# Packed turns of q, two loads behind a broadcast, and two reordered exps in a fused attention and feed-forward kernel

## The chip, the cores and the metric

The kernel runs on one core of one Trainium2 chip. The metric is the device time of an execution in microseconds (us). Engines are named as in the profile: PE is TensorE, PEld its weight loads, DVE VectorE, ACT ScalarE, POOL GpSimd, and SP the queue that issues transfers. A profile of one execution gives the span, from the first to the last instruction, which is some 2 us shorter than that time, and a trace of every instruction and transfer.

## The reference

Linformer attention (8 batches, 8 heads, 1024 rows, head size 64) feeds a maxout feed-forward block:

```python
k_proj = einsum('ks,bhsd->bhkd', E, k)          # 64 projected rows
v_proj = einsum('ks,bhsd->bhkd', F, v)
scores = q @ k_proj.T / 8
attn   = exp(scores - max); attn /= attn.sum(-1)
x      = (attn @ v_proj) -> [8192, 512]
h      = maximum(maximum(x @ w1, x @ w2), x @ w3)   # 512 -> 768
out    = h @ w_out                                   # 768 -> 512
```

## The kernel before

Instructions are issued in a hand-made order: while TensorE does the feed-forward of batch b, the attention of batch b+1 is slipped in between steps. A step (0, 3) is the fourth of ten in the first half of a batch; steps 0 to 5 are column groups of w1, w2, w3, steps 6 to 9 are output projections. PSUM has eight banks; `bank()` and `two()` hand out the bank (or pair) that the model of time thinks free first.

The parts that matter (cuts marked):

```python
def load(b, which):                      # q, k, v of batch b: float32 in HBM -> bf16, on the GpSimd queue
    ...
        dma = nc.gpsimd.dma_start(out=tiles[i], in_=view((q, k, v)[i], b))
        if i == 0 and b - 1 in last_T:   # q waits for the q transposes of the batch before
            after(dma, last_T[b - 1])

def heads_q(b, g, sis, t):               # turns of q for batch 0: half-width transposes on TensorE
    for i, si in enumerate(sis):
        for hp in range(2):
            nc.tensor.transpose(out=t[hp*HALF:(hp+1)*HALF, i*P:(i+1)*P],
                                in_=qkv[b][0][:, 2*g + hp, si, :], identity=ident)

def zc(b, queue=nc.sync):                # 1 / row sums of a whole batch
    ...  # sums on TensorE; Ln and Exp on ScalarE -> zic
        nc.sync.dma_start(out=zd..., in_=zic...)           # 32 KB to DRAM
        for u in range(2):
            for hp in range(2):
                queue.dma_start(out=zi_all(b)[...], in_=zd[gs, hp].partition_broadcast(HALF))

def qd(b, parts=1):                      # q of the other batches: packed on VectorE, turned by DMA
    ...
        last_T[b] = nc.sync.dma_start_transpose(out=qTs[b][...], in_=q_p[...])

def sc(b, g, lo=0, nsi=SI, now=False):   # scores; the exp follows now, or after the next h1 copy
    ...
def up(b, ch, jt, mid=None):             # one column group of w1, w2, w3
    ...
    nc.scalar.copy(out=h1s, in_=h[0][0])
    run_later()                          # postponed exps
    nc.vector.tensor_tensor(out=m12, in0=h[1][0], in1=h1s, op=ALU.max)
    most(hTs[b, ch][:, jt, :], *h[2], m12)
```

`vx(b, g)` multiplies the values by `zi_all` into `xT`, the input of the feed-forward; `za` does sums, inverse and values of one head pair.

The softmax here doesn't subtract the row's maximum and nothing guards it: scores larger than these inputs give would overflow.

Of the kernel before, what the change touches and what calls it, by code (L numbers as in the profile page):

```python
# [15 lines left out]
def kernel(  # L16
# [231 lines left out]
    def zc(b, queue=nc.sync):  # L248



        def f():
            t, ns = bank()
            for hp in range(2):
                for g in range(NPAIR):
                    nc.tensor.matmul(  # L256
                        out=t[32 * g:32 * (g + 1), :], lhsT=pick[:, hp, :],
                        rhs=pTs[b, g, 0][:, hp, :], start=(hp == 0), stop=(hp == 1),
                    )
            ready = pe(2 * MM + 0.1)  # L260
            zlc = att.tile([P, CHUNK], FP32, name="zlc", bufs=1)
            nc.scalar.activation(out=zlc, in_=t, func=AF.Ln)
            runs("s", ready, 0.6, ns)
            zic = att.tile([P, CHUNK], FP32, name="zic", bufs=1)
            nc.scalar.activation(out=zic, in_=zlc, func=AF.Exp, scale=-1.0)
            when = runs("s", ready, 0.63) + 9.0
            zd = scratch.tile([NPAIR, 2, 2, CHUNK], FP32, name="zd")
            nc.sync.dma_start(
                out=zd.rearrange("g h c f -> (g h c) f"),
                in_=zic.rearrange("(a r) f -> a r f", r=8)[:, 0, :],  # L270
            )
            for u in range(2):
                gs = slice(2 * u, 2 * u + 2)
                for hp in range(2):
                    queue.dma_start(
                        out=zi_all(b)[hp * HALF:(hp + 1) * HALF, gs],
                        in_=zd[gs, hp].partition_broadcast(HALF),
                    )
            for g in range(NPAIR):
                zis[b, g, 0] = zi_all(b)[:, g], when  # L280
        return f
# [39 lines left out]
    def sc(b, g, lo=0, nsi=SI, now=False):  # L321
        def f():
            t = scores(b, g, lo, nsi)
            if now:
                exps(b, g, lo, nsi, t)
            else:
                later.append(lambda: exps(b, g, lo, nsi, t))
        return f

    def za(b, g, lo=0, nsi=SI, then=False):  # L330
        def f():
            z = sums(b, g, lo, nsi)
            av = values(b, g, lo, nsi)
            invert(b, g, lo, nsi, z)
            if then:
                later.append(lambda: scale_x(b, g, lo, nsi, av))
            else:
                scale_x(b, g, lo, nsi, av)
        return f
# [13 lines left out]
    def heads_q(b, g, sis, t):  # L353
        for i, si in enumerate(sis):
            for hp in range(2):
                nc.tensor.transpose(
                    out=t[hp * HALF:(hp + 1) * HALF, i * P:(i + 1) * P],
                    in_=qkv[b][0][:, 2 * g + hp, si, :],
                    identity=ident,
                )  # L360
        pe(0.08 * len(sis))

    def qp(b, gs, lo=0, nsi=SI):
        def f():
            if b not in qTs:
                qTs[b] = att.tile([P, NPAIR * SI, P], BF16, name="qT")
            t, ns = two()
            t = t.bitcast(BF16)[:, 0]
            n = nsi * P
            for i, g in enumerate(gs):  # L370
                heads_q(b, g, range(lo, lo + nsi), t[:, i * n:(i + 1) * n])
            o = qTs[b].rearrange("a (g si) p -> a g si p", si=SI)
            copy(
                "v", o[:, gs[0]:gs[-1] + 1, lo:lo + nsi, :],
                t[:, 0:len(gs) * n].rearrange("a (g si p) -> a g si p", si=nsi, p=P),
                ns, 0.1 + len(gs) * nsi * 0.08,
            )
        return f
# [20 lines left out]
    def kproj(b):  # L399
        def f():  # L400
            t, ns = bank()
            proj(b, 1, t, (LO, HI), 4 * D)
            kps[b] = att.tile([P, 2, 2 * D], BF16, name="kp")
            copy("v", kps[b].rearrange("a g x -> a (g x)"), t[:, 0:4 * D], ns, 0.43)
        return f
# [18 lines left out]
    def vproj(b):  # L424
        def f():
            t, ns = bank()
            proj(b, 2, t, (LO, HI), 4 * D)

            vps[b] = att.tile([P, H, D], BF16, name="vp")
            for hh, hs in enumerate((LO, HI)):  # L430
                i = t[hh * HALF:(hh + 1) * HALF, 0:4 * D].rearrange("a (h d) -> a h d", d=D)
                for to in range(2):
                    copy("sv"[hh], vps[b][to * HALF:(to + 1) * HALF, hs, :], i, ns, 0.4)
        return f
# [247 lines left out]
    def ld(b, which=(0, 1, 2)):  # L682
        return lambda: load(b, which)

    def plan(b):
        n = b + 1
        if b == 0:
            c1 = (SPC, SPC)
            return {
                (0, 6): [za(0, 1, *c1), sc(0, 3, *c1)],  # L690
                (0, 7): [qd(1, 2), za(0, 2, *c1)],
                (0, 8): [za(0, 3, *c1)],
                (1, 0): [kproj(1)],
                (1, 1): [kt(1)],
                (1, 2): [vproj(1), ld(2)],
                (1, (3, "mid")): [sc(1, 0), sc(1, 1)],
                (1, 4): [za(1, 0), sc(1, 2)],
                (1, 5): [za(1, 1), sc(1, 3)],
                (1, 7): [za(1, 2)],
                (1, 8): [za(1, 3)],  # L700
            }
        if b == 1:
            return {
                (0, 0): [qd(2)],
                (0, 3): [kproj(2), vproj(2), ld(3, (0, 1))],
                (0, 4): [kt(2)],
                (0, 5): [sc(2, 0, now=True), sc(2, 1, now=True), sc(2, 2)],
                (0, 6): [sc(2, 3)],
                (0, 8): [zc(2, nc.gpsimd), ld(3, (2,))],
                (1, 1): [qd(3)],  # L710
                (1, 3): [vx(2, 0), vx(2, 1)],
                (1, 6): [vx(2, 2), vx(2, 3)],
            }
        if b == 2:
            return {
                (0, 1): [kproj(3), vproj(3), ld(4)],
                (0, 2): [kt(3)],
                (0, 3): [sc(3, 0, now=True), sc(3, 1)],
                (0, 5): [sc(3, 2, now=True), sc(3, 3)],
                (0, 7): [zc(3)],  # L720
                (0, 8): [qd(4)],
                (1, 3): [kproj(4), vproj(4), ld(5), vx(3, 0), vx(3, 1)],
                (1, 4): [kt(4)],
                (1, 6): [vx(3, 2), vx(3, 3), sc(4, 0)],
            }
        if n == B:
            return {}
        out = {
            (0, 1): [sc(n, 1, now=True), sc(n, 2, now=True), sc(n, 3)],
            (0, 3): [zc(n)],  # L730
            (1, 2): [vx(n, 0), vx(n, 1)],
            (1, 6): [vx(n, 2), vx(n, 3)],
        }
        if n + 1 < B:
            out[0, 4] = [qd(n + 1)]
            out[1, 2] = [kproj(n + 1), vproj(n + 1)] + out[1, 2]
            out[1, 3] = [kt(n + 1)]
            out[1, 6] += [sc(n + 1, 0)]
        if n + 2 < B:
            out[1, 3] += [ld(n + 2)]  # L740
        return out

    for b in range(B):
        p = plan(b)

        def behind(ch, step):
            for f in p.get((ch, step), []):
                f()

        for ch in range(NCHUNK):  # L750
            if (b, ch) == (0, 0):
                c1 = (SPC, SPC)
                up_first({
                    (0, 0, 5): [lambda: v_pair(2)],
                    (0, 1, 2): [lambda: x(2)],
                    (0, 1, 5): [lambda: v_pair(3), ld(1)],
                    (0, 2, 2): [lambda: x(3)],
                    (2, "a", 2): [qp(0, (0, 1), *c1)],
                    (2, "a", 4): [qp(0, (2, 3), *c1)],
                    (2, 0): [sc(0, 0, *c1)],  # L760
                    (2, 2): [sc(0, 1, *c1)],
                    (2, 4): [za(0, 0, *c1, then=True), sc(0, 2, *c1)],
                })
                run_later()
                behind(0, NJT - 1)
            else:
                for step in range(NJT):
                    up(b, ch, step, lambda: behind(ch, (step, "mid")))
                    behind(ch, step)
            for tt in range(SPC):  # L770
                down(b, ch, tt, "v" if b == 0 else "s")
                behind(ch, NJT + tt)
# [30 lines left out]
```

## Time and profile before

Three executions took 403.04, 403.15 and 403.41 us; the profiled one took 402.78 and spans 401.0 us. This is the head of its page (busy time, share of the span, count) and the chain of waits by engine:

```profile
span 401.0 us, 5737 instructions
PE 388.7 (97%) x2261; PEld 176.7 (44%) x2303; DVE 203.3 (51%) x319; ACT 149.0 (37%) x238; POOL 34.1 (9%) x48
...
PE 80%; DMA 11%; DVE 3%; issue 2%; ACT 2%; POOL 1%; DVEq 0%; ACTq 0%; POOLq 0%
```

TensorE is busy 97% of the time, at a granted clock of 1.00. Only its waits can be won. From 28 us on, the view of waits of TensorE shows these (total, times, longest). A wait "on issue" of 0.16 us stands where a matmul record is missing, and is none.

```profile
PE banks L664 <- issue: 0.8, 5, 0.2
PE banks L567 <- issue: 0.8, 5, 0.2
PE banks L664 <- DVE hT L577: 0.7, 1, 0.7
PE banks L231 <- DVE xT L308: 0.3, 1, 0.3
PE banks L345 <- DMA v_t<-in_v_dram: 0.3, 1, 0.3
PE banks L567 <- DVE xT L308: 0.2, 1, 0.2
```

The largest, 0.7 us, is the end of a story that the timeline tells (start, duration, engine, operation; in brackets the idle time before it and what ended it; SPq and POOL lines are issues of transfers):

```profile
88.50 0.89 POOL L200 DMA_DIRECT2D k_t<-in_k_dram  x1
...
99.76 0.53 SPq L268 DMA_DIRECT2D zd<-zic  x1
104.81 2.58 POOL L275 DMA_DIRECT2D zi_all<-zd  x4 [15.42 <-DMA zd<-zic]
107.39 0.91 POOL L200 DMA_DIRECT2D v_t<-in_v_dram  x1
112.63 2.35 DVE L308 TENSOR_TENSOR xT<-banks,zi_all 128x1024 bf16<-128x1024 f32 x2 [1.70 <-PE banks L567]
117.83 0.39 PE L664 MATMUL banks<-wout_sb,hT 128*128 128x512 bf16 x1 [0.70 <-DVE hT L577]
```

A load of k occupies the DMA engines (16.0 us to landing); the tiny zd write needs 4.5 us; the broadcast starts late, so VectorE idles 1.70 us, then is late with hT.

Two more places, the turns of q with the first output projection, and the projection of v of batch 1. The first line, of a projection of v of batch 0, serves below as a mark:

```profile
20.52 0.61 PE L496 MATMUL banks<-v_t,efT 128*128 128x128 bf16 x8
...
33.02 0.64 PE L356 MATMUL banks<-ident,q_t 128*64 128x128 bf16 x16
33.59 1.04 PE L567 MATMUL banks<-xT,w_sb 128*128 128x512 bf16 x4
...
34.56 0.64 PE L356 MATMUL banks<-ident,q_t 128*64 128x128 bf16 x16
...
39.60 1.46 PE L664 MATMUL banks<-wout_sb,hT 128*128 128x512 bf16 x6
...
55.95 1.06 PE L345 MATMUL banks<-v_t,efT 128*64 128x256 bf16 x16 [0.32 <-DMA v_t<-in_v_dram]
```

Sixteen half-width transposes hold TensorE 0.57 us (33.02 to 33.59). At 55.95 it has been waiting for a transfer that was issued at 25.75 and took 30.2 us.

### The profile page before, as it was taken

To read this page: it belongs to the slowest core of one execution; us is meant where nothing else is said; L and a number is where in the kernel's file an instruction comes from. 1 tells how busy PE (TensorE), PEld (TensorE's weight loads), DVE (VectorE), ACT (ScalarE), POOL (GpSimd) and SP (SyncE) were. 2 spreads that over 40 slices of the span, in tenths; PEclk is the share of its full clock that TensorE was granted. 3 is DMA by queue.
4 is the path that set the end of the run, shared out by engine and by line. 5 is a ranking of instruction groups with operands and counts; after the bars stand their busy time and mean duration, and the time that the engine had idled before them with its cause. 6 is when DMAs were issued, how large, how long until landed. Compare 5 with 4: busy or idle time off the path is not lost.

```text
span 401.0 us, 5737 instructions
## 1 busy us (share of the span) xinstructions
PE 388.7 (97%) x2261; PEld 176.7 (44%) x2303; DVE 203.3 (51%) x319; ACT 149.0 (37%) x238; POOL 34.1 (9%) x48
## 2 busy tenths in 40 slices
PE   7899999999999999999999999999999999999996
PEld 3444444353435435444454445444454444444443
DVE  3348755761673525826274544744267342745251
ACT  2622537527213452253323542245323533132312
POOL 7340002010301000200020000200000000000000
PEclk9999999999999999999999999999999999999999
DMA  9999999969799989999899959992890229020202
GB/s 157 206 205 207 231 202 156 240 137 187 222 183 253 191 171 209 174 227 181 205 222 180 236 122 217 211 235 63 203 217 2 105 65 252 3 106 0 105 2 105
DMA packets 66315, 66.11 MB, mean 165 GB/s; under 512 B 30608, under 2 KB 58768, under 8 KB 66288
## 3 DMA queue, kind: packets, MB, share of 16 engines
q0 software_dynamic: 29088, 30.41, 47.2%
q1 hardware_dynamic: 37056, 35.20, 34.9%
q8 instruction: 18, 0.29, 0.3%
q10 hardware_dynamic: 144, 0.13, 0.1%
q14 instruction: 9, 0.07, 0.1%
HBM read 69.73 MB, written 16.97 MB: 216 GB/s over the span
## 4 chain that ended last, share of the span: by engine, by line
PE 80%; DMA 11%; DVE 3%; issue 2%; ACT 2%; POOL 1%; DVEq 0%; ACTq 0%; POOLq 0%
PE banks L567 54%; PE banks L664 18%; DMA v_t<-in_v_dram 8%; DMA w_sb<-in_moe_w_dram 3%; PE banks L345 3%; PE banks L231 2%; DVE xT L308 2%; PE banks L211 2%; PE banks L256 1%; ACT zi_all L297 1%; ACT zl L291 1%; DVE m L629 1%; DVE hT L577 0%; POOL k_t L152 0%; POOL q_t L157 0%
## 5 line engine op out<-in xcount | busy, mean ns | idle before, releaser
L567 PE MATMUL banks<-xT,w_sb 128*128 128x512 bf16 x1119 | 254.8, 379 | 3.8 <-DMA w_sb<-in_moe_w_dram 1.3
L567 PEld LDWEIGHTS <-w_sb 128*128 128x128 bf16 x1152 | 110.0, 98 | 137.5 <-issue 8.7
L629 DVE TENSOR_TENSOR m<-banks,h1s 128x512 f32<-128x512 f32 x90 | 62.1, 690 | 135.7 <-ACT h1s L625 92.4
L625 ACT COPY h1s<-banks 128x512 f32<-128x512 f32 x90 | 52.6, 585 | 119.7 <-PE banks L567 119.6
L664 PE MATMUL banks<-wout_sb,hT 128*128 128x512 bf16 x370 | 85.8, 379 | 1.7 <-issue 0.8
L577 DVE TENSOR_TENSOR hT<-banks,m 128x512 bf16<-128x512 f32 x90 | 62.3, 692 | 10.4 <-PE banks L567 0.8
L664 PEld LDWEIGHTS <-hT 128*128 128x128 bf16 x378 | 35.3, 98 | 48.8 <-issue 5.8
L102 ACT COPY o_sb<-banks 128x512 f32<-128x512 f32 (+1 forms) x56 | 32.6, 582 | 58.7 <-PE banks L664 58.3
L222 ACT ACTIVATE pT<-banks 128x1024 bf16<-128x1024 f32 (+1 forms) x36 | 32.7, 932 | 25.3 <-PE banks L211 25.3
L308 DVE TENSOR_TENSOR xT<-banks,zi_all 128x1024 bf16<-128x1024 f32 x28 | 33.2, 1220 | 12.0 <-PE banks L231 5.5
L200 POOL DMA_DIRECT2D q_t<-in_q_dram x7 | 6.1, 877 | 192.9 <-DMA qT<-q_p 102.4
L102 DVE CAST vp<-banks 64x256 bf16<-64x256 f32 (+1 forms) x18 | 7.1, 397 | 12.4 <-ACT vp L102 8.8
L345 PEld LDWEIGHTS <-efT 128*64 128x64 bf16 x224 | 11.6, 110 | 3.8 <-issue 3.0
L102 ACT CAST vp<-banks 64x256 bf16<-64x256 f32 x14 | 5.1, 364 | 20.7 <-PE banks L345 20.6
L231 PE MATMUL banks<-pT,vp 64*64 64x512 bf16 (+1 forms) x144 | 11.4, 363 | 0.4 <-DVE vp L102 0.4
L211 PE MATMUL banks<-qT,kpT 64*64 64x512 bf16 (+1 forms) x144 | 11.2, 361 | 0.0
L291 ACT ACTIVATE zl<-banks 128x512 f32<-128x512 f32 (+1 forms) x12 | 8.9, 739 | 5.2 <-PE banks L231 4.4
L102 DVE COPY q_p<-q_t 128x1024 bf16<-128x1024 bf16 x28 | 10.1, 425 | 0.0
L102 DVE COPY o_sb<-banks 128x512 f32<-128x512 f32 (+1 forms) x9 | 5.8, 654 | 4.5 <-PE banks L644 4.5
L441 PE MATMUL banks<-warm_f 128*128 128x512 f32 x8 | 6.6, 977 | 1.5 <-DVE warm_f L175 1.5
L345 PE MATMUL banks<-v_t,efT 128*64 128x256 bf16 x112 | 7.3, 273 | 0.3 <-DMA v_t<-in_v_dram 0.3
L345 PE MATMUL banks<-k_t,efT 128*64 128x256 bf16 x112 | 7.5, 276 | 0.0
(60 smaller groups left out, 119.0 us busy)
## 6 DMA issues: line engine op xcount, KB each, us to landing
out_dram<-o_sb SPq DMA_DIRECT2D x30, 512.0 KB, 5.0
zi_all<-zd SPq DMA_DIRECT2D x20, 512.0 KB, 7.9
q_t<-in_q_dram POOLq DMA_DIRECT2D x7, 1024.0 KB, 9.5
k_t<-in_k_dram POOLq DMA_DIRECT2D x7, 1024.0 KB, 16.0
v_t<-in_v_dram POOLq DMA_DIRECT2D x7, 1024.0 KB, 21.1
zi_all<-zd POOLq DMA_DIRECT2D x4, 512.0 KB, 8.0
w_sb<-in_moe_w_dram POOLq DMA_DIRECT2D x5, 384.0 KB, 12.6
k_t<-in_k_dram POOLq DMA_DIRECT2D x2, 512.0 KB, 8.8
```

The costliest lines, as they stand in the source:

```text
L102: done = {"v": nc.vector.tensor_copy, "s": nc.scalar.copy, "g": nc.gpsimd.tensor_copy}[eng](out=o, in_=i)
L211: nc.tensor.matmul(out=t[c * HALF:(c + 1) * HALF, hp, 0:n * P], lhsT=kpTs[b][rows, g, :], rhs=qTs[b][rows, at:at + n, :], start=True, stop ...
L222: nc.scalar.activation(out=pTs[b, g, lo], in_=t, func=AF.Exp, scale=scale)
L231: nc.tensor.matmul(out=t[hp * HALF:(hp + 1) * HALF, c, 0:nsi * HALF], lhsT=w(rows, hp), rhs=p[rows, hp, :], start=True, stop=True,)
L291: nc.scalar.activation(out=zl, in_=t, func=AF.Ln)
L308: nc.vector.tensor_tensor(out=xTs[b][:, g, lo:lo + nsi, :].rearrange("a (c s) p -> a c (s p)", c=2), in0=t, in1=zi, op=ALU.mult,)
L345: nc.tensor.matmul(out=t[hh * HALF:(hh + 1) * HALF, 0:width], lhsT=efT[:, si, (kv - 1) * KP:kv * KP], rhs=qkv[b][kv][:, heads[hh], si, :], ...
L567: nc.tensor.matmul(out=h, lhsT=w_sb[i][:, ct, jt * P:(jt + 1) * P], rhs=xTs[b][:, ct, ch * SPC:(ch + 1) * SPC, :], start=(ct == first), st ...
L577: nc.vector.tensor_tensor(out=o, in0=h, in1=other, op=ALU.max)
L625: nc.scalar.copy(out=h1s, in_=h[0][0])
L629: nc.vector.tensor_tensor(out=m12, in0=h[1][0], in1=h1s, op=ALU.max)
L664: nc.tensor.matmul(out=o_ps, lhsT=hTs[b, ch][:, jt, tt * P:(tt + 1) * P], rhs=wout_sb[:, jt, :], start=(jt == 0), stop=(jt == NJT - 1),)
```

## The change

The intent has four parts. (1) Pack q of batch 0 on VectorE so that a turn is eight full-width transposes in place of sixteen, and put the turns later so that the packing is done. (2) Keep k of batch 3 out of the way of the zd write. (3) Run the exps of batch 1 before the h1 copy, so that score banks come free sooner. (4) Put the values of batch 3 and the first scores of batch 4 one step later.

```diff
+    def pack_q(b, gs, lo, nsi):
+        def f():
+            if b not in q_pk:
+                q_pk[b] = att.tile([P, NPAIR, SI, 2, D], BF16, name="q_p", bufs=1)
+            for g in gs:
+                copy("v", q_pk[b][:, g, lo:lo + nsi]..., qkv[b][0][:, 2 * g:2 * g + 2, lo:lo + nsi], (), 0.25)
+        return f
     def qp(b, gs, lo, nsi):
-                heads_q(b, g, range(lo, lo + nsi), t[:, i * n:(i + 1) * n])
+                for si in range(nsi):
+                    nc.tensor.transpose(out=t[...], in_=q_pk[b][:, g, lo + si]..., identity=ident)
... (batch 0)
-                (1, (3, "mid")): [sc(1, 0), sc(1, 1)],
-                (1, 4): [za(1, 0), sc(1, 2)],
+                (1, (3, "mid")): [sc(1, 0, now=True), sc(1, 1)],
+                (1, 4): [za(1, 0), sc(1, 2, now=True)],
... (batch 1)
-                (0, 3): [kproj(2), vproj(2), ld(3, (0, 1))],
+                (0, 3): [kproj(2), vproj(2), ld(3, (0,))],
-                (0, 8): [zc(2, nc.gpsimd), ld(3, (2,))],
+                (0, 8): [zc(2, nc.gpsimd), ld(3, (1, 2))],
... (batch 2)
-                (1, 6): [vx(3, 2), vx(3, 3), sc(4, 0)],
+                (1, 7): [vx(3, 2), vx(3, 3), sc(4, 0)],
... (batch 0, third weight)
-                    (2, "a", 2): [qp(0, (0, 1), *c1)],
-                    (2, "a", 4): [qp(0, (2, 3), *c1)],
-                    (2, 0): [sc(0, 0, *c1)],
-                    (2, 2): [sc(0, 1, *c1)],
+                    (2, "a", 0): [pack_q(0, (0, 1), *c1)],
+                    (2, "a", 1): [pack_q(0, (2, 3), *c1)],
+                    (2, "a", 4): [qp(0, (0, 1), *c1)],
+                    (2, "a", 5): [qp(0, (2, 3), *c1)],
+                    (2, 1): [sc(0, 0, *c1)],
+                    (2, 3): [sc(0, 1, *c1)],
```

More of the change, by code (lines that the diff above doesn't have):

```diff
@@ L361, in heads_q, with qp @@
         pe(0.08 * len(sis))
-    def qp(b, gs, lo=0, nsi=SI):
+    q_pk = {}
+    def pack_q(b, gs, lo, nsi):
         def f():
-            if b not in qTs:
-                qTs[b] = att.tile([P, NPAIR * SI, P], BF16, name="qT")
+            if b not in q_pk:
+                q_pk[b] = att.tile([P, NPAIR, SI, 2, D], BF16, name="q_p", bufs=1)
+            for g in gs:
+                copy(
+                    "v", q_pk[b][:, g, lo:lo + nsi].rearrange("p si h d -> p h si d"),
+                    qkv[b][0][:, 2 * g:2 * g + 2, lo:lo + nsi], (), 0.25,
+                )
+        return f
+    def qp(b, gs, lo, nsi):
+        def f():
             t, ns = two()
@@ L370, in f @@
             for i, g in enumerate(gs):
-                heads_q(b, g, range(lo, lo + nsi), t[:, i * n:(i + 1) * n])
+                for si in range(nsi):
+                    nc.tensor.transpose(
+                        out=t[:, i * n + si * P:i * n + (si + 1) * P],
+                        in_=q_pk[b][:, g, lo + si].rearrange("p h d -> p (h d)"),
+                        identity=ident,
+                    )
+                pe(0.06 * nsi)
             o = qTs[b].rearrange("a (g si) p -> a g si p", si=SI)
```

## The prediction

> **What bounds the kernel.** TensorE. The page shows it busy 388.7 of 401.0 us (97%) at a granted clock of 1.00; the chain of waits is 80% TensorE, 11% DMA. Its idle time is 12.3 us in all, 4.0 in the first 20 us (busy time by stage). The change removes almost no matmul work, so it can only recover small waits.
>
> **1. Packed turns of q.** Before: 32 half-width transposes, 16 in 0.57 us, twice (from 33.02 and 34.56 in the timeline). After: 16 full-width ones; the two of kp take 0.11 us, so eight cost about 0.44 (estimate): 0.26 us less TensorE. Added: four pack copies on VectorE, each half a q_p copy (0.36-0.42 us), 0.8 us together; VectorE idles about 1.4 us there. But only two matmuls (0.43 us) now separate the turns, where four did, and both turns use the same PSUM pair: the second waits for the first 0.69 us qT copy, about 0.4 us. Net near zero, and absorbed anyway: v of batch 1, issued at 25.75, lands at 55.95, and TensorE already waits 0.32 us for it (chain, timeline). That load is not moved. Worth 0 (-0.2 to +0.2).
>
> **2. k and v of batch 3 behind the broadcast.** Before, k of batch 3 (issued at 88.50, 16 us to landing) fills the DMA engines when the 32 KB zd write goes out at 99.76; that takes 4.5 us against a 2.4 median, the broadcast starts at 104.81, and VectorE idles 1.70 us before the first xT at 112.63. TensorE loses 0.76 us in 110-120, 0.70 of it waiting for hT at 117.83. After: broadcast about 2.4 us earlier, xT starts when its matmuls end, that 0.7 goes. Price: k (about 6.5 us of DMA time, from q and k in 15.5) joins v and the q transposes in 105-127, where DMA shows 9s. The Trainium skill, page "DMA: Bandwidth & Descriptors", section "Queues, rings and completion order", says that each DMA engine alternates between its queues by packets; the trace agrees (both queues move data in 116-124). I put the landing of v at 127.5-130, was 124.4; TensorE wants it near 128. Expected stall 0.5, possibly 2.
>
> **3. First exps of batch 1 ahead of the h1 copy.** ScalarE: exp 0.97 us, h1s 0.58. The copy of step 3 moves from 58.0 to about 60; the next matmuls have other banks. At 66.4-67.4 TensorE now loses about 0.5 us waiting for banks (xT, then m). After, the sums wait less (0.2) but the scores of group 3 wait for a later h1s and m. Net -0.3 to +0.2.
>
> **4. Values of batch 3 one place later.** xT copies leave the way of the last hT; the first down group there spans 1.71 us against 1.46 elsewhere. Gain 0.25.
>
> **Sum.** 0.7 + 0.25 - 0.5 - 0.1: some 0.4 us less; a little more for interactions: 402.5 us, range 401.2 to 403.9. Chances: faster by over 2% 0.01, within 2% 0.98, slower by over 2% 0.01.
>
> **What would show it.** (1) TensorE idles 0.3-0.5 us before the second turn; vproj of batch 1 still begins within 0.3 us of 55.95. (2) zd lands in about 2.5 us, broadcast issued near 102.4, no hT wait near 117; v of batch 3 lands after 127, with a TensorE wait for v_t if I am right about contention. (3) h1s of step 3 near 60; idle TensorE near 66-67 similar. (4) That down group near 1.46 us.
>
> **What would make it wrong.** v of batch 1 landing at another time (then part 1 comes through whole); v of batch 3 late by over 2 us; q transposes of batch 3 landing after 134, where its scores are wanted; new waits from another bank order in batches 4 to 7.

## The result, and the profile after

The changed kernel took 402.8 us (median of 4; 402.4 to 403.25), the one before 403.1 (median of 4). The ratio is 0.9993, with a 95% interval of 0.9976 to 1.001. Ratios here are the mean time of one kernel's fast runs over that of the other's in the same rounds, so not quite the ratio of the medians. The time alone cannot tell the change from nothing; the profiled span is 400.6 us against 401.0.

The head of the page after, and the waits of TensorE from 28 us on (line numbers of the feed-forward are 19 higher: L586 was L567, L683 was L664):

```profile
span 400.6 us, 5751 instructions
PE 391.9 (98%) x2287; PEld 176.6 (44%) x2287; DVE 204.1 (51%) x323; ACT 148.8 (37%) x238; POOL 33.9 (8%) x48
...
PE 89%; DMA 3%; DVE 3%; ACT 2%; issue 1%; POOL 1%; DVEq 0%; ACTq 0%; POOLq 0%
```

```profile
PE banks L211 <- ACT zl L291: 0.5, 1, 0.5
PE banks L385 <- DVE qT L102: 0.3, 1, 0.3
PE banks L211 <- DVE m L648: 0.3, 1, 0.3
PE banks L586 <- DVE xT L308: 0.2, 1, 0.2
```

The hT wait, the v_t wait and the wait of L231 for xT (0.3 us) are gone, and three new ones have come. (Busy time rose by 3.2 us though TensorE has less to do: the trace before lacks some matmul records and this one lacks none, so busy times of the two must not be compared.) The broadcast:

```profile
100.28 0.53 SPq L268 DMA_DIRECT2D zd<-zic  x1
102.66 2.36 POOL L275 DMA_DIRECT2D zi_all<-zd  x4 [13.62 <-DMA zd<-zic]
105.00 0.92 POOL L200 DMA_DIRECT2D k_t<-in_k_dram  x1
105.89 0.92 POOL L200 DMA_DIRECT2D v_t<-in_v_dram  x1
111.37 2.35 DVE L308 TENSOR_TENSOR xT<-banks,zi_all 128x1024 bf16<-128x1024 f32 x2
116.40 1.46 PE L683 MATMUL banks<-wout_sb,hT 128*128 128x512 bf16 x6
```

The zd write landed 1.8 us after its issue, VectorE goes into xT without idling, and the six matmuls take 1.46 us with no wait. The mark, the turns and the projection of v of batch 1:

```profile
20.48 0.61 PE L515 MATMUL banks<-v_t,efT 128*128 128x128 bf16 x8
...
33.75 0.61 PE L385 MATMUL banks<-ident,q_p 128*128 128x128 bf16 x8
34.20 0.59 PE L586 MATMUL banks<-xT,w_sb 128*128 128x512 bf16 x2
34.40 0.69 DVE L102 COPY qT<-banks 128x1024 bf16<-128x1024 bf16 x1 [0.21 <-PE banks L385]
...
35.14 0.61 PE L385 MATMUL banks<-ident,q_p 128*128 128x128 bf16 x8 [0.35 <-DVE qT L102]
...
39.57 0.30 PE L211 MATMUL banks<-qT,kpT 64*64 64x256 bf16 x4 [0.52 <-ACT zl L291]
...
40.25 1.46 PE L683 MATMUL banks<-wout_sb,hT 128*128 128x512 bf16 x6
...
56.21 1.06 PE L345 MATMUL banks<-v_t,efT 128*64 128x256 bf16 x16
```

A turn now takes 0.45 us (33.75 to 34.20) in place of 0.57. But the second waits 0.35 us for its banks and the scores of group 2 wait 0.52 for theirs. The output projection begins 0.65 us later than before, and yet the projection of v only 0.26 us later. (v landed at 54.7 us here, before TensorE came; in the profile before it landed at 55.9, and TensorE waited.)

To follow where time goes I cut the TensorE timeline at five places and took the lengths between. Lengths do not carry over the start: six profiles with identical code up to 39 us (before, p2_only, p3_only, p4_only, p2p4, p24_mid) reach the first output projection anywhere from 39.19 to 40.07 us. Each length is the difference of two starts in the timeline, in us:

| kernel | first output projection at | to k projection of batch 2 | to values of batch 2, group 2 | to k projection of batch 4 | to scores of batch 4, group 1 | span |
|---|---|---|---|---|---|---|
| before | 39.60 | 45.40 | 33.15 | 40.03 | 19.32 | 401.0 |
| changed | 40.25 | 45.27 | 32.27 | 40.04 | 19.31 | 400.6 |
| p1_only | 40.28 | 45.02 | 33.15 | 40.04 | 19.31 | 401.3 |
| p2_only | 40.07 | 45.02 | 32.27 | 40.04 | 19.67 | 400.5 |
| p3_only | 39.58 | 45.75 | 33.11 | 40.04 | 19.31 | 401.3 |
| p4_only | 39.72 | 45.02 | 33.53 | 40.03 | 19.32 | 401.1 |
| p2p4 | 39.19 | 45.67 | 32.27 | 40.03 | 19.32 | 399.9 |
| no_p4 | 40.36 | 45.27 | 32.26 | 40.05 | 19.87 | 401.3 |
| pk_act | 38.92 | 45.76 | 32.27 | 40.04 | 19.31 | 399.8 |
| pk_mid | 39.41 | 44.95 | 32.26 | 40.17 | 19.31 | 399.6 |
| p24_mid | 39.81 | 44.94 | 32.27 | 40.04 | 19.31 | 399.8 |

So the changed kernel loses 0.65 us by 40 us, gains 0.13 in the next stretch and 0.88 in the third, and nothing after.

The first column and the span hold the start as well as the change. The scatter of the start lies before the mark, a projection of v of batch 0 that begins at 20.11 to 21.00 us: from there to the first output projection it is 19.07 to 19.08 us in all six profiles with the old turns, 19.76 to 19.77 in the four with the turns of the change (changed, p1_only, no_p4, k_extra) and 18.70 in pk_act and pk_mid. So the new turns cost 0.69 us. The next stretch holds chance too. From the first output projection to the projection of v of batch 1 it is 15.96 us wherever that projection is in its old place and TensorE does not wait for v. With the old turns it is 16.35 in the profile before, 15.96 in p2_only and p4_only, 16.44 in p3_only and 16.61 in p2p4: the same code waits 0 to 0.65 us. Spans of single profiles therefore do not decide between forecasts a few tenths apart; waits and lengths do.

The experiments below say which part does what.

### The profile page after: what moved, and what is told of

Its sections match the earlier page's. It is cut to its first block, busy times and chain, and to the rows that moved or that the text cites. A ratio compares the mean times of both kernels' runs of the same rounds, so it can differ in the third digit from the quotient of the medians.

```text
span 400.6 us, 5751 instructions
## 1 busy us (share of the span) xinstructions
PE 391.9 (98%) x2287; PEld 176.6 (44%) x2287; DVE 204.1 (51%) x323; ACT 148.8 (37%) x238; POOL 33.9 (8%) x48
## 4 chain that ended last, share of the span: by engine, by line
PE 89%; DMA 3%; DVE 3%; ACT 2%; issue 1%; POOL 1%; DVEq 0%; ACTq 0%; POOLq 0%
PE banks L586 60%; PE banks L683 20%; PE banks L345 3%; DMA w_sb<-in_moe_w_dram 3%; PE banks L231 2%; PE banks L211 2%; DVE xT L308 1%; PE banks L256 1%; ACT zl L291 1%; DVE hT L596 1%; ACT zi_all L297 1%; DVE m L648 0%; POOL k_t L152 0%; POOL q_t L157 0%; POOL v_t L152 0%
## 5 line engine op out<-in xcount | busy, mean ns | idle before, releaser
L586 PE MATMUL banks<-xT,w_sb 128*128 128x512 bf16 x1152 | 257.5, 379 | 1.4 <-DMA w_sb<-in_moe_w_dram 1.1
L586 PEld LDWEIGHTS <-w_sb 128*128 128x128 bf16 x1152 | 110.1, 98 | 137.3 <-issue 8.7
L683 PE MATMUL banks<-wout_sb,hT 128*128 128x512 bf16 x378 | 86.9, 380 | 0.1
L683 PEld LDWEIGHTS <-hT 128*128 128x128 bf16 x378 | 35.3, 98 | 47.6 <-issue 5.8
L102 ACT CAST vp<-banks 64x256 bf16<-64x256 f32 x14 | 5.1, 364 | 20.3 <-PE banks L345 20.2
L231 PE MATMUL banks<-pT,vp 64*64 64x512 bf16 (+1 forms) x144 | 11.5, 364 | 0.4 <-DVE vp L102 0.4
L102 DVE COPY q_p<-q_t 128x1024 bf16<-128x1024 bf16 (+1 forms) x32 | 11.3, 415 | 0.0
```

Source lines behind the costliest of these rows:

```text
L102: done = {"v": nc.vector.tensor_copy, "s": nc.scalar.copy, "g": nc.gpsimd.tensor_copy}[eng](out=o, in_=i)
L231: nc.tensor.matmul(out=t[hp * HALF:(hp + 1) * HALF, c, 0:nsi * HALF], lhsT=w(rows, hp), rhs=p[rows, hp, :], start=True, stop=True,)
L586: nc.tensor.matmul(out=h, lhsT=w_sb[i][:, ct, jt * P:(jt + 1) * P], rhs=xTs[b][:, ct, ch * SPC:(ch + 1) * SPC, :], start=(ct == first), st ...
L683: nc.tensor.matmul(out=o_ps, lhsT=hTs[b, ch][:, jt, tt * P:(tt + 1) * P], rhs=wout_sb[:, jt, :], start=(jt == 0), stop=(jt == NJT - 1),)
```

## The experiments

Theory: part 2 is the only gain, 0.88 us; parts 1 and 3 lose, and the loss of part 1 is partly swallowed, because the wait for v of batch 1 goes; part 4 does nothing by itself. The rivals: the parts simply add, or part 4 and the loads matter in another way.

### p2_only: the loads alone

```diff
-                (0, 3): [kproj(2), vproj(2), ld(3, (0, 1))],
+                (0, 3): [kproj(2), vproj(2), ld(3, (0,))],
-                (0, 8): [zc(2, nc.gpsimd), ld(3, (2,))],
+                (0, 8): [zc(2, nc.gpsimd), ld(3, (1, 2))],
```

> Only the reordered loads of batch 3 (k and v behind the broadcast); everything else as before. Theory (parts interact by the landing of v): the hT wait near 117.8 goes, so TensorE gains 0.7 to 0.9 us by 118; but v of batch 3 lands near 128.2 whatever TensorE does, and TensorE, not delayed by parts 1 and 3, arrives at that projection near 127.9 us, so it now waits 0.2 to 0.5 us for v_t. Span 400.3 to 400.6, against 401.0 before. Rival (the parts simply add): no wait for v_t, span 400.1, the whole 0.87 us kept.

Measured: 402.39 us (6 runs) against 402.68; ratio 0.9994 (0.9977 to 1.0011); span 400.5. There was no wait for v_t: v was issued at 105.48, landed 22.2 us later at 127.7, and TensorE came at 127.98. So the expected wait missed by 0.3 us. The 0.88 us appears in the third stretch. But 0.35 us comes back as a loss in the last stretch, which neither theory had foreseen:

```profile
167.56 0.41 PE L211 MATMUL banks<-qT,kpT 64*64 64x512 bf16 x4 [0.16 <-DMA qT<-q_p]
```

The first scores of batch 4 wait for the q transposes, which landed at 167.5 (issued at 154.12, 13.4 us to landing; before, 152.46 plus 14.1, which is 166.6). The bracket shows 0.16; the whole delay is seen in the distance from the first of the values just before, at 166.77, to this line: 0.79 us, where it was 0.46 before (167.55 to 168.01). The load of q of batch 4 was issued at 130.98 where it was at 127.55, since it waits for the q transposes of batch 3. These now share the DMA engines with k as well as v, and landed at 130.4 where they had landed at 127.0.

### p1_only: the packed turns alone

The edit is the first and the last part of the diff above.

> Only the packed turns. Theory: TensorE is 0.6 us later at the first matmul of the first output projection (near 40.25 against 39.60 us), from a wait of 0.35 for the second turn's banks and 0.5 for the scores of group 2, and only 0.25 to 0.3 us later after the projection of v of batch 1, which now lands earlier than 55.9 and is not waited for. Span about 401.2 to 401.3. Rival (absorbed wholly, as I predicted): no change after 56 us, span 401.0.

Measured: 403.35 us (4 runs), ratio 1.002 (1.0001 to 1.0038), span 401.3. The waits in TensorE from 28 to 60 us:

```profile
PE banks L211 <- ACT zl L291: 0.5, 1, 0.5
PE banks L385 <- DVE qT L102: 0.4, 1, 0.4
```

The first output projection begins at 40.28, the projection of v of batch 1 at 56.24, with no wait for v_t. The theory holds against this profile of the kernel before: of 0.68 us lost by 40 us (0.69 counted from the mark), 0.29 is left at 56 us, and to the end. My prediction that all of it is swallowed does not hold. What gave 0.39 back is the wait for v: the stretch was 16.35 us with it and is 15.96 without (the bracket before shows 0.32 of it). As this wait was 0 to 0.65 us in other profiles of the same code, what is left of part 1 at 56 us is 0.04 to 0.69 us, depending on the execution it is held against; the times, 0.2% apart with an interval just clear of 1, fit anywhere there. The landing of v is not fixed: v took 29.3 us here and 30.2 before. Over the twelve profiles it took 29.2 to 29.6 us in the four where the q transposes of batch 1 were issued at 45.3 us or later, and 29.9 to 30.3 in the eight where they were issued by 45.2. These four are also the four kernels with the turns of the change, and no run moved the q transposes alone, so why v landed sooner is not shown. (The packing alone is not enough: pk_act and pk_mid pack too, and have 30.2 and 29.9.)

### p3_only: the exps alone

```diff
-                (1, (3, "mid")): [sc(1, 0), sc(1, 1)],
-                (1, 4): [za(1, 0), sc(1, 2)],
+                (1, (3, "mid")): [sc(1, 0, now=True), sc(1, 1)],
+                (1, 4): [za(1, 0), sc(1, 2, now=True)],
```

> Only the exps of batch 1 ahead of the h1 copy. Theory: the wait near 66.8 shrinks but the scores of group 3 wait for m, 0.25 us net loss by 72 us, kept to the end: span 401.2. Rival (its cost in the changed kernel came from the shift by part 1): no loss, span 401.0.

Measured: 402.98 us (4 runs), ratio 1.001 (0.9991 to 1.003), span 401.3. The theory holds: after the projection of v (56.02, which waited 0.41 us for v_t) TensorE reaches the k projection of batch 2 29.31 us later, where it was 29.05 before (29.05 to 29.06 in every profile with the old exps and the projection of v in its old place, 29.31 in all four with the new exps). The new wait:

```profile
67.06 0.37 PE L211 MATMUL banks<-qT,kpT 64*64 64x512 bf16 x1
67.70 0.41 PE L211 MATMUL banks<-qT,kpT 64*64 64x512 bf16 x3 [0.27 <-DVE m L629]
```

The scores of group 3 wait for m, and m was late because its h1 copy now stands behind an exp of 1.0 us. Two things are in the net loss: the sums just before no longer wait for xT, which won 0.35 us, and the second of these score matmuls begins 0.64 us after the first, where it was 0.16 before.

### p4_only: the later values alone

```diff
-                (1, 6): [vx(3, 2), vx(3, 3), sc(4, 0)],
+                (1, 7): [vx(3, 2), vx(3, 3), sc(4, 0)],
```

> Only the values of groups 2 and 3 of batch 3 and the first scores of batch 4, one place later. Theory: the last hT of that half is issued before these in any case, so nothing changes: the sixth output matmul still waits 0.2 us for hT near 167, span 401.0, TensorE arrives at batch 3's first matmul at the same time (172.2). Rival (my prediction): the wait goes and the span falls by 0.25.

Measured: 402.64 us (4 runs), ratio 0.9995 (0.9972 to 1.0019), span 401.1. No gain: the last stretch is 19.32 us as before. The last hT comes after the xT copies of groups 0 and 1, which were not moved; the moved ones are issued after it and cannot have delayed it.

The third stretch grew by 0.38, and that is worth a look. TensorE came 0.26 us earlier to the k projection of batch 2 in this run, yet the values are 0.12 us later. The zd write was issued at 99.50 and took 5.1 us to land. In the four profiles with the early load of k, zd was issued from 99.50 to 100.09, took 4.5 to 5.1 us, and the broadcast began at 104.81 to 105.39. So this place seems tied to the load of k, not to when TensorE arrives, and an early TensorE only waited longer (0.96 us for hT here).

### p2p4: parts 2 and 4

> The reordered loads and the later values of batch 3, without the packed turns and without the exps ahead of h1. Theory: part 2 keeps its 0.8 us because the scores of batch 4, one place later, no longer wait for the q transposes (they waited 0.33 us with part 2 alone): no TensorE wait for qT, span 400.0 to 400.2. Rival (the 0.35 us lost between 158 and 177 us with part 2 alone has another cause): span 400.5 as with part 2 alone.

Measured: 401.98 us (6 runs) against 403.29; ratio 0.9966 (0.9944 to 0.9988); span 399.9. No wait for qT; the last stretch is 19.32 again. The theory holds, and it gives part 4 its meaning: by itself it does nothing, but it takes the first scores of batch 4 out of the way of a transfer that part 2 makes later. This version is faster than the kernel before, clear of noise, by 0.34%. Some of that ratio may be luck of these rounds: the lengths in the table explain 0.88 us, which is 0.22% and inside the interval, and one of the executions of the kernel before took 405.52 us at a granted clock of 0.991. The span of 399.9 has luck as well: this profile came to the mark 0.41 us earlier than the one before, and then waited 0.65 us for v of batch 1.

### no_p4: the changed kernel without part 4

> The changed kernel with part 4 undone. Theory: the first scores of batch 4 are reached near 167.2 us but the q transposes of batch 4 land near 168.0, so TensorE waits 0.6 to 0.9 us for qT; span 401.1 to 401.4. Rival (part 4 does nothing, as when it is alone): span 400.6, no wait for qT.

Measured: span 401.3, one time of 403.12 (one run, state unknown).

```profile
168.30 0.41 PE L211 MATMUL banks<-qT,kpT 64*64 64x512 bf16 x4 [0.37 <-DMA qT<-q_p]
```

The last stretch is 19.87, which is 0.56 us longer than with part 4. The direction and cause hold; the size is just under the expected 0.6 to 0.9.

### k_extra: half of k loaded once more

```diff
+            t = loads.tile([P, H // 2, SI, D], BF16, name="spare", bufs=1)
+            nc.gpsimd.dma_start(out=t, in_=view(k, b)[:, LO])
...
-                (0, 8): [zc(2, nc.gpsimd), ld(3, (1, 2))],
+                (0, 8): [zc(2, nc.gpsimd), ld(3, (1,)), extra(3), ld(3, (2,))],
```

> The changed kernel with half of k of batch 3 loaded a second time, into a spare tile, between k and v (same results). Theory (v of batch 3 lands when the DMA engines have got through what is queued, with 0.1 us to spare in the changed kernel): v lands 3.3 to 4.6 us later and TensorE waits 3 to 4.5 us for v_t at its projection; span 403.5 to 405.5. Rival (a long latency but spare DMA time in that stretch): v lands at most 1.5 us later, wait at most 1.5 us, span under 402.2.

Measured: the result is correct; span 407.7, one time of 409.7 (one run, state unknown). v was issued at 106.74 and landed 26.2 us later, at 132.9 (changed kernel: 105.89 plus 22.4, which is 128.3, and TensorE came at 128.41). The wait is the one expected:

```profile
127.61 1.06 PE L345 MATMUL banks<-k_t,efT 128*64 128x256 bf16 x16
132.99 1.92 PE L345 MATMUL banks<-v_t,efT 128*64 128x256 bf16 x16 [4.32 <-DMA v_t<-in_v_dram]
134.84 4.33 PE L586 MATMUL banks<-xT,w_sb 128*128 128x512 bf16 x11
```

So the changed kernel had 0.1 us to spare, and half of k more in that stretch cost a wait of 4.3 us. But the span grew by 7.1 us, more than the 4.3 us wait. The busy time by stage shows why; after the length of the stretch come busy times and counts of PE, PEld, DVE, ACT and POOL, then the granted TensorE clock (the last two columns, of the DMA engines, are not used here):

```profile
127.00:131.00 4.00, 1.68 (x20) 0.89 (x17) 1.74 (x3) 0.00 (x0) 0.00 (x0) 1.00 1.21 195
131.00:133.00 2.00, 0.01 (x2) 0.01 (x2) 0.00 (x0) 0.00 (x0) 0.00 (x0) 0.56 1.25 203
133.00:135.00 2.00, 2.00 (x17) 1.37 (x18) 0.00 (x0) 0.04 (x1) 0.07 (x1) 0.50 1.16 384
135.00:137.00 2.00, 2.00 (x6) 0.65 (x5) 0.85 (x2) 0.92 (x3) 2.00 (x3) 0.50 0.71 245
137.00:139.00 2.00, 1.95 (x7) 0.80 (x7) 0.58 (x1) 0.35 (x1) 0.56 (x1) 0.73 1.01 132
139.00:141.00 2.00, 2.00 (x12) 0.99 (x11) 1.00 (x3) 0.58 (x1) 0.00 (x0) 1.00 1.18 188
```

The clock fell to half during the wait and came back only after some 5 us of work. The clock records of the trace have it at half from 131.23 to 138.06, which is 6.83 us, twice 3.41. TensorE had stopped at 128.68 and resumed at 132.99, so 2.6 us of idling came before the fall and 5.1 us of work before the release. The sixteen matmuls on v took 1.92 us in place of 1.04, and from this projection to the k projection of batch 4 it was 31.87 us in place of 29.42: the half clock cost about 2.45 us, most of the rest of the 7.1. The Trainium skill, page "TensorE: Matmul & The Clock Gate", section "Part 1: The HAM clock gate (the "warmup" mystery)", says that the clock is throttled to 4/8 after an idle window of about 3.4 us and released after a busy one of about that length, and that these windows run freely and do not start with the kernel. The trace agrees on the half, and the 5.1 us of work before the release lie between one such window and two. That 2.6 us of idling were enough for the fall does not fit a window of 3.4 us that is idle throughout.

### pk_act: the packing on ScalarE, turns where they were

Parts 2 and 4, and part 1 with these differences (part 3 left out):

```diff
-                    "v", q_pk[b][:, g, lo:lo + nsi]...
+                    "s", q_pk[b][:, g, lo:lo + nsi]...
-                    (2, "a", 0): [pack_q(0, (0, 1), *c1)],
-                    (2, "a", 1): [pack_q(0, (2, 3), *c1)],
-                    (2, "a", 4): [qp(0, (0, 1), *c1)],
-                    (2, "a", 5): [qp(0, (2, 3), *c1)],
-                    (2, 1): [sc(0, 0, *c1)],
-                    (2, 3): [sc(0, 1, *c1)],
+                    (2, "a", 0): [pack_q(0, (0, 1, 2, 3), *c1)],
+                    (2, "a", 2): [qp(0, (0, 1), *c1)],
+                    (2, "a", 4): [qp(0, (2, 3), *c1)],
+                    (2, 0): [sc(0, 0, *c1)],
+                    (2, 2): [sc(0, 1, *c1)],
```

> Parts 2 and 4, and packed turns whose pack copies run on ScalarE (idle from 27 to 36 us) at the places the turns had before, so that four matmuls stand between the two turns. Theory: no wait for the second turn's banks nor for zl at the scores of group 2; first output projection begins 0.26 us earlier than before (about 39.3); but the q transposes of batch 1 start earlier, v of batch 1 lands at 55.8 to 56.1 and TensorE waits 0.4 to 0.7 us for it: span 400.0 to 400.2, equal to parts 2 and 4 alone within 0.15. Rival (the turns' gain is kept): span 399.8 to 399.9.

Measured: 402.22 us (6 runs), ratio 0.9987 (0.996 to 1.0014), span 399.8. The packing took 2.18 us of idle ScalarE time. No wait for the turn's banks, none for zl. The gain is swallowed as the theory says:

```profile
55.63 1.06 PE L345 MATMUL banks<-v_t,efT 128*64 128x256 bf16 x16 [0.68 <-DMA v_t<-in_v_dram]
```

The projection of v begins at 55.63 where p2p4 has 55.80, though pk_act was 0.27 us ahead at the first output projection; and its load of v had been issued 0.15 us earlier. Counted from the mark, the packed turns won 0.38 us over the kernel before (18.70 against 19.08). The rival (gain kept, span 399.8) cannot be excluded by the span, only by this wait.

### pk_mid and p24_mid: the projection of v of batch 1 later

Both move it by eight matmuls, pk_mid on top of pk_act and p24_mid on top of p2p4:

```diff
-                (1, 2): [vproj(1), ld(2)],
-                (1, (3, "mid")): [sc(1, 0), sc(1, 1)],
+                (1, (3, "mid")): [vproj(1), sc(1, 0), sc(1, 1), ld(2)],
```

> pk_act with the projection of v of batch 1 moved by eight matmuls (1.73 us), into the middle of step 3 just ahead of the scores, so that v of batch 1 has landed when TensorE comes to it. Theory (that landing is what took back every gain made before 56 us): no wait for v_t near 56, the 0.7 us that pk_act waited there is kept, span 399.0 to 399.3 against pk_act's 399.8. Rival (another limit stands right behind, the banks near 66 or the loads of batch 2): the gain is gone again by 85 us, span 399.6 to 399.8.

> Parts 2 and 4 with the same move of the projection, turns as before. Theory: no wait for v_t near 56; span 399.3 to 399.7, and 0.2 to 0.3 us above pk_mid, which is the packed turns' gain, now kept. Rival: no difference between the two, or no gain over parts 2 and 4 alone (399.9).

Measured, on one chip: pk_mid 401.55 us (5 runs) against 402.56, ratio 0.9975 (0.9961 to 0.9988), span 399.6; p24_mid 401.60 us, ratio 0.9979 (0.9966 to 0.9991), span 399.8. No wait for v_t near 56 in either. The stretch to the k projection of batch 2 fell to 44.95 and 44.94 us, from 45.76 in pk_act and 45.67 in p2p4. So the wait was what took the gains back, as the theory says, and 0.7 to 0.8 us are won in that stretch. The expected span of pk_mid (399.0 to 399.3) was missed: its profile reached the first output projection 0.49 us later than that of pk_act, all of it before the mark. The difference between the two, 0.05 us in the medians, is too small for the times to show. The traces show more: from the mark to the k projection of batch 2 it is 63.64 us in pk_mid and 64.02 in p24_mid, so the 0.38 us of the packed turns is still there at 84 us; pk_mid then loses 0.13 of it on the way to the k projection of batch 4 (40.17 against 40.04). Both beat the kernel before; which of p2p4, pk_mid and p24_mid is the best was not measured.

## Why the prediction was right or wrong

The time, 402.8 us, lay in the range and near the 402.5 foretold. That says little for the mechanism: the range of 2.7 us also held the unchanged kernel's 403.1, and the measured difference is not clear of noise. Of the terms of the sum, some were off and cancelled, which is luck.

- Part 2's gain, put at 0.7 us, was 0.88, and the mechanism was as described: zd landed in 1.8 us (about 2.5 foretold), the broadcast was issued at 102.66 (102.4), the hT wait was gone.
- Part 2's price, "Expected stall 0.5", was zero in the changed kernel. The landing of v at 128.3 us was within the foretold 127.5 to 130; TensorE came 0.1 us after it. k_extra showed that the contention is real.
- A price of part 2 was missed: the q transposes of batch 3 end later (130 us and over), q of batch 4 is loaded 3 us later, and its transposes are late for the first scores of batch 4. It cost 0.35 us in p2_only, 0.56 in no_p4, and nothing in the changed kernel, thanks to part 4. (The prediction feared these transposes for the scores of batch 3; the price came at those of batch 4.)
- Part 1, "Worth 0 (-0.2 to +0.2)", cost 0.69 us by 40 us, of which 0.30 is left at 56 us against this profile of the kernel before, both counted from the mark. The transposes (0.12 us less per turn) and the first wait (0.35) were as foretold. Missed was the wait of 0.52 us for zl: zl reads the sums just before, so the scores of group 2 had got the pair of banks of these sums. Also wrong was that the landing of v is fixed, though the prediction named this as what would make it wrong. v landed 1.2 us sooner in the changed kernel (0.8 in p1_only), and TensorE no longer met it.
- Part 3, put at about -0.1 (a loss), cost 0.26 us, by the cause named: scores waiting for a later h1 copy and m.
- Part 4, "Gain 0.25", gave none by itself, and in the changed kernel the sixth matmul of that group still begins 0.24 us late. The step that failed is "xT copies leave the way of the last hT": the moved copies are issued after that hT. Its use was for the transfer above.

Summed from the mark: 0.30 and 0.26 lost (65.03 us to the k projection of batch 2 against 64.48), 0.88 won; with 0.04 us of a sooner start that is, to rounding, the 0.36 us that TensorE is early from 118 us to the end. The large change moved little because one part's gain was more than half spent by two others.

That v landed sooner where the q transposes started later is in keeping with the Trainium skill, page "DMA: Bandwidth & Descriptors", section "Issuing engines are not separate DMA queues": transfers of all issuers run on the same 16 DMA engines and interleave. It is a pattern over the profiles here, not an experiment made for it, and stays open. The other open point is the start: why profiles of identical code come to the mark at 20.11 to 21.00 us was not studied; their waits for the first loads differ (for k 0.6 us in the profile before, 1.2 in p2_only).

## What to carry to other kernels

Ask of every wait whether it is tied to the instruction order or to a transfer; a gain upstream of a transfer that lands at its own time is only a longer wait, until the consumer is moved behind it. When you move a load, follow what its traffic delays, to the next batch. Count lengths from a mark behind the scatter of the start, or it passes for an effect. And test the parts of a change one by one and in pairs: a part that does nothing alone can be the one that protects another's gain.

## What the Trainium skill lacked or had wrong

- Page "DMA: Bandwidth & Descriptors", section "Queues, rings and completion order": it gives round-robin between queues by packets. How much one busy queue delays a small transfer on another is not there: a 32 KB write landed in 1.8 us with k out of the way and in 4.5 to 5.1 us beside its load.
- Same page: it gives a bandwidth of DMA transposes, but neither it nor another page says how long one takes beside other traffic. The 1 MB transposes of q of batch 3 took 19.7 to 20.3 us to land beside v, and 22.0 to 23.2 beside k and v (25.9 with half of k once more).
- Page "TensorE: Matmul & The Clock Gate", section "Part 4: PE-mode transpose": it gives some 275 ns for a 128x128 transpose in a kernel, and does not say how closely transposes follow each other. Here the record of a full-width one was 216 to 219 ns long, but eight of them began 56 ns apart and held TensorE 0.45 us. Sixteen half-width ones went in pairs, whose two began within 4 ns of each other; the pairs were 56 ns apart too (some 80 after the first), and held it 0.57 us. So packing to full width saved 0.12 us in 0.57, not half.
- Same page, section "Part 1: The HAM clock gate (the "warmup" mystery)": borne out on the half clock. Its idle window of about 3.4 us does not fit the fall here, which came 2.6 us after TensorE stopped. A single wait of 4.3 us so became a loss of 7.1 us in the span; waits of up to 0.96 us left the clock at 1.00.
